# RWKV attention and two MLP layers: weights converted a slot at a time, bonus diagonals and decay clamp on GpSimd, and a new order of the first 24 steps

## The chip, the cores and the metric

The kernel runs on one core of a Trainium2 chip. The metric is device time in microseconds (us), one launch, everything from the first instruction to the last store. TensorE is called PE below, VectorE DVE, ScalarE ACT, GpSimd POOL, and SyncE's queue, which issues every DMA here, SP.

## The reference

A recurrent attention (4 batches, 8 heads, 768 tokens, head size 48) feeds a gated layer (384 to 1536 to 384) and then a squared-ReLU layer (384 to 2048 to 384), over 3072 tokens:

```python
for t in range(S):
    cur = einsum('bhd,bhe->bhde', u[None] * kt, vt)
    y[:, :, t] = einsum('bhd,bhde->bhe', rt, state + cur)
    state = wt[:, :, :, None] * state + einsum('bhd,bhe->bhde', kt, vt)
x = y laid out as (B*S, H*D)
x = (sigmoid(x @ w_gate) * (x @ w_val)) @ w_out
h = x @ w_in
out = (relu(h) ** 2) @ w_out2
```

The weights arrive as 64-bit floats in memory (the kernel sees pairs of 32-bit words); tokens and decays are float32.

## The kernel before

**Attention by chunks.** Each batch is cut into 6 chunks of 128 tokens, so there are 24 chunks; four of them (one of each batch) make a group of 512 tokens, and there are six groups. The steps of a chunk have one letter each in the order that the kernel keeps: L loads it (two DMAs, `att` with r, k and the decays w, `tok` with r, k, v by token); S is the scan on DVE (L318 clamps the decays in place, L319 and L324 are the two prefix scans, L327 scales r and k); B multiplies r, k and u on POOL (L342, L343); R sums that by head on DVE (L349) and writes eight diagonal 128x128 matrices on ACT (L355); A makes the r-k products on PE (L379) and copies their triangle over the diagonals on DVE (L382); K transposes k (L363, L368); D decays the carried state (L334, L337); Y makes the output on PE (L394, L400) and splits it into a high and a low half (L62, L63); U updates the state (L414, L421); G counts decays out of bounds on ACT (L300).

**First layer.** For each group there are 12 steps f, numbered through from 0 to 71. Step i has P (gate projection, 9 matmuls of 128x512 columns on L427 to L429, then the sigmoid on ACT, L457), Q (value projection, 9 matmuls, the product on DVE, L462, and its rounded copy on ACT, L463), l (the low half on DVE, L467) and M (9 matmuls into three accumulators). All products are made three times, with high and low halves of weights and data.

**Weights.** The 12 slots of weights w0 to w11 hold three parts of 384 columns each, high and low. Before, a part is a unit: 36 units, each loaded into one of 4 `raw` buffers (L154). A tick (letter T) of the stream runs, for three units at different stages: on ACT an Abs with a sum and a Relu with a sum (L166, L167, which count values out of bounds; each is followed by a reading of the accumulator); on DVE three integer instructions that put a float32 together out of the two words (L176, L181, L186); and the split, a rounding copy on ACT (L137) and a subtraction on POOL (L138). P of step i needs unit 3i, Q unit 3i+1, M unit 3i+2. Slots w7 to w11 first serve as space for chunks 2 and 3.

**Second layer's weights** are 32 units: stream s2 (ticks t) converts them in groups 2 to 4 in the same way (here with a clamp, L163 and L174) and stores them to memory as float32; r ticks in group 5 load them back and split them.

**Order.** Every engine runs its queue in program order, and that order is written by hand: the text START lists the steps for chunks 0 to 12 and f steps 0 to 23, and `steady` lists those of the other groups. In `steady` a chunk's B comes behind a Q, its scan behind the l that follows, its R at the end of that f step, and A and K behind the next Q. At the start SP issues chunks 0 to 3 with the first three weight units between them (L492 to L503).

Of the kernel before, what the change touches and what calls it, by code (L numbers as in the profile page):

```python
# [16 lines left out]
C = 128  # L17
# [18 lines left out]
    S0 B0 s0 T W19 R0 A0 S1 G0 T B1 K0 Y0 B2 S2 T R1 A1 U0 K1 K2 R2 G1 U1 S3 L4 B3 U2 T Y1 A2 K3 R3 A3 T L5 Y2  # L36
    G2 Y3 G3 U3 S4 T B4 Z P0 T R4 Q0 G4 D4 T A4 P1 K4 l0 T Q1 T Y4 l1 U4 S5 T P2 L6 M0 T M1 B5 T K5 Q2 R5 T T
    P3 l2 T A5 D5 Q3 P4 M2 T T l3 T Q4 T l4 Y5 G5 T U5 M3 T P5 Q5 T M4 S6 P6 l5 T B6 T Q6 D6 P7 T R6 M5 L7 T
    A6 K6 Q7 l6 T Y6 T l7 U6 T T P8 M6 T Q8 P9 l8 G6 M7 B7 S7 T D7 Q9 M8 T R7 A7 T L8 T P10 Y7 K7 G7 Q10 l9
    P11 l10 T U7 B8 T S8 M9 Q11 D8 M10 l11 P12 R8 M11 L9 Q12 P13 A8 K8 l12 Q13 M12 Y8 l13 G8 S9 B9 D9 U8 P14  # L40
    Q14 M13 P15 Q15 l14 P16 l15 M14 Q16 L10 B10 l16 M15 R9 A9 K9 P17 G9 Q17 S10 Y9 U9 l17 R10 P18 M16 Q18 M17
    P19 D10 L11 G10 l18 A10 Q19 B11 S11 P20 D11 Y10 R11 l19 K10 M18 Q20 U10 P21 M19 G11 L12 Q21 l21 l20 A11
    B12 S12 P22 M20 Q22 Y11 l22 K11 P23 U11 M21 R12 Q23 l23 M22 L13
# [22 lines left out]
def rwkv_moe(tc, att, tok, vt, u, w1, w2, out):  # L66
# [3 lines left out]
    with ExitStack() as ctx:  # L70
# [18 lines left out]
        outside = sb.tile([128, 2 * len(ORDER) + 6 * F1], F32, name="outside")  # L89
        out_w, out_s, out_b = (  # L90
            outside[:, 0 : 2 * len(ORDER)],
            outside[:, 2 * len(ORDER) : 2 * len(ORDER) + 3 * F1],
            outside[:, 2 * len(ORDER) + 3 * F1 :],
        )
        junk = sb.tile([128, DM], F32, name="junk")
# [33 lines left out]
        def w_part(i, part):  # L129
            k = i // 3  # L130
            if k not in wtile:
                wtile[k] = sb.tile([128, 2, 3, DM], F32R, name=f"w{k}", tag=f"w{k}")
            return wtile[k][:, part, i % 3]

        def w_split(i, val, eng):
            hi = w_part(i, 0)
            nc.scalar.copy(hi, val)  # L137
            eng.tensor_tensor(out=w_part(i, 1), in0=val, in1=hi.bitcast(F32), op=ALU.subtract)  # L138

        class Unit:  # L140
# [6 lines left out]
            def __init__(self, src, done, note=None):  # L147
                self.src, self.done, self.note = src, done, note

            def load(self):  # L150
                shape, dt = ([128, DM, 2], I32) if wide else ([128, DM], F32)
                self.raw = sb.tile(shape, dt, name="raw", tag="raw", bufs=4)
                src = self.src.bitcast(I32).rearrange("p (a b) -> p a b", b=2) if wide else self.src
                nc.sync.dma_start(self.raw, src)  # L154

            def start(self):
                if not wide:
                    self.h = self.raw
                    return
                self.h = sb.tile([128, DM], F32, name="h", tag="h", bufs=4)  # L160
                high = self.raw[:, :, 1].bitcast(F32)
                if self.note is None:
                    nc.scalar.activation(self.h, high, AF.Abs)  # L163
                else:
                    n = slice(self.note, self.note + 1)
                    nc.scalar.activation(junk, high, AF.Abs, accum_out=out_b[:, n])  # L166
                    nc.scalar.activation(junk, junk, AF.Relu, bias=1.0, scale=-1.0 / TINY, accum_out=out_s[:, n])  # L167

            def step(self, n):
                if not wide:  # L170
                    return
                h, hi = self.h, self.h.bitcast(I32)
                if n == 0 and self.note is None:
                    nc.vector.tensor_scalar(out=h, in0=h, scalar1=TINY, scalar2=HUGE, op0=ALU.max, op1=ALU.min)  # L174
                elif n == 1:
                    nc.vector.tensor_scalar(  # L176
                        out=hi, in0=hi if self.note is None else self.raw[:, :, 1], scalar1=3, scalar2=0x3FFFFFFF,
                        op0=ALU.logical_shift_left, op1=ALU.bitwise_and,
                    )
                elif n == 2:  # L180
                    nc.vector.scalar_tensor_tensor(  # L181
                        out=hi, in0=self.raw[:, :, 0], scalar=29, in1=hi,
                        op0=ALU.logical_shift_right, op1=ALU.bitwise_or,
                    )
                elif n == 3:
                    nc.vector.scalar_tensor_tensor(  # L186
                        out=hi, in0=self.raw[:, :, 1], scalar=-0x40000000, in1=hi,
                        op0=ALU.bitwise_and, op1=ALU.bitwise_or,
                    )

        class Stream:


            def __init__(self, units, lag):
                self.u, self.n, self.k, self.lag = units, 0, 0, lag
# [6 lines left out]
            def tick(self):  # L202
                k, u, lag = self.k, self.u, self.lag
                if k >= len(u) + lag + 2:
                    return
                self.k += 1
                at = lambda n: [u[n]] if 0 <= n < len(u) else []
                for x in at(k - lag - 2):
                    x.done(x.h)
                self.fetch(k + 1)  # L210
                for x in at(k):
                    x.start()
                mid, old = at(k - lag), at(k - lag - 1)
                for x in mid:
                    x.step(0)
                for x in old:
                    x.step(2)
                for x in mid:
                    x.step(1)
                for x in old:  # L220
                    x.step(3)
                self.fetch(k + 3)

            def until(self, n):
                while self.k < min(n, len(self.u)) + self.lag + 2:
                    self.tick()

        def w1_unit(i, note=None):
            src = w1[i // 3, :, DM * (i % 3) : DM * (i % 3) + DM]
            return Unit(src, lambda h: w_split(i, h, nc.gpsimd), note)  # L230

        def w2_unit(i):
            return Unit(w2[i // 2, :, DM * (i % 2) : DM * (i % 2) + DM], lambda h: nc.sync.dma_start(w2f[i], h))

        s1 = Stream([w1_unit(i, i) for i in range(3 * F1)], 0)
        s2 = Stream([w2_unit(i) for i in range(2 * F2)] if wide else [], 1)

        class Refill:
# [5 lines left out]
            def tick(self):  # L244
                if self.k >= 2 * F2:
                    return
                for i in range(self.k, min(self.k + 3, 2 * F2)):
                    if i not in self.t:
                        self.t[i] = sb.tile([128, DM], F32, name="h", tag="h", bufs=4)
                        src = w2f[i] if wide else w2[i // 2, :, DM * (i % 2) : DM * (i % 2) + DM]  # L250
                        nc.sync.dma_start(self.t[i], src)
                w_split(self.k, self.t.pop(self.k), nc.gpsimd)
# [41 lines left out]

        def st_guard(i):
# [16 lines left out]
        def st_scan(i, p0, p1):  # L312
# [4 lines left out]
            wc = wz[:, fl].rearrange("p (a c) -> p a c", c=CW)[:, :, 1 : C + 1]  # L317
            nc.vector.tensor_scalar(out=wc, in0=wc, scalar1=W_LOW, scalar2=W_HIGH, op0=ALU.max, op1=ALU.min)  # L318
# [26 lines left out]
        def st_bonus2(i):  # L345
# [3 lines left out]
            nc.vector.reduce_sum(out=a0, in_=d["t"][:, 0:DM].rearrange("p (h e) -> p h e", e=D), axis=AX.X)  # L349
            if spare(i):  # L350
                d["am"] = [spare(i)[:, n : n + 512].rearrange("p (a b) -> p a b", b=C) for n in (0, 512)]
            else:
                d["am"] = [sb.tile([128, NP, C], F32, name=f"am{i}_{j}", tag=f"am{j}", bufs=1) for j in range(2)]
            for h in range(H):
                nc.scalar.mul(d["am"][h % 2][:, h // 2], ident, a0[:, h : h + 1])  # L355
# [166 lines left out]
        def load(i):  # L522
# [4 lines left out]
            S=lambda i: half(i, 0), s=lambda i: half(i, 1), D=st_decay, G=st_guard, A=st_a, K=st_kt, B=st_bonus, R=st_bonus2,  # L527
# [14 lines left out]
        def st_p(i):  # L542
            if i < F1:
                s1.until(3 * i + 1)
# [3 lines left out]
        def st_q(i):  # L548
            if i < F1:
                s1.until(3 * i + 2)  # L550
# [3 lines left out]
        def st_m(i):  # L554
            if i < F1:
                s1.until(3 * i + 3)
# [20 lines left out]
        def steady(g):  # L577

            work = [[[], [], [], []] for _ in range(F1 + 1)]
            if g + 1 < NG:  # L580
                n = len(GROUPS[g + 1])
                for j, i in enumerate(GROUPS[g + 1]):
                    k = F1 // n * j
                    if k > 0:
                        work[k - 1][1] += ["B", i]
# [8 lines left out]
                    if j == n - 1 and i + 1 < len(ORDER):  # L594
                        work[F1 - 1][1] += ["B", i + 1]
# [3 lines left out]
            for f in range(F1):  # L599
                if NG - 4 <= g < NG - 1:  # L600
                    work[f][3] += ["t", 0]
# [28 lines left out]
        class Slot2:  # L630
# [18 lines left out]
            def mix(self):  # L649
                hi, lo = w_part(2 * self.f + 1, 0), w_part(2 * self.f + 1, 1)  # L650
                b0, b1 = self.f == 0, self.f == F2 - 1
                for j in range(4):
# [5 lines left out]
                    if b1:  # L658
                        y = sb.tile([128, DM], F32, name="y", tag="h", bufs=4)
# [93 lines left out]
        def general():  # L753
            scan_attention()
            wtile.clear()
            again = Stream([w1_unit(i) for i in range(3 * F1)], 1)
# [28 lines left out]
def lay_out(i):  # L785
# [29 lines left out]
    w2 = np.concatenate([cols(i["moe2_w_in"], F2), np.asarray(i["moe2_w_out"]).reshape(F2, 128, DM)], 2)  # L815
# [21 lines left out]
```

## Time and profile before

| | us |
|---|---|
| median of 3 runs | 1056.22 (1054.44 to 1056.26) |
| the profiled execution | 1050.92 |
| its span | 1049.1 |
| mean granted PE clock in it | 0.971 of full speed |

The span is what the profile covers; the profiled execution took 1.8 us more than its span. In the profile, "busy" counts the time in which an instruction stands in an engine, its waiting for a memory port included. L numbers are lines of the kernel before.

### The profile page before, as it was taken

How to read it: one execution, taken by the hardware profiler on the slowest of the kernel's cores; microseconds unless marked ns; L12 is line 12 of the kernel's file. 1: busy time of each engine (PE TensorE's matmuls, PEld its weight loads, DVE VectorE, ACT ScalarE, POOL GpSimd, SP SyncE). 2: the span in 40 equal slices, each digit the busy share in tenths (PEclk: the TensorE clock that was granted, in tenths of full speed). 3: DMA queues.
4: the chain of work that ended last, by engine and by line, in shares of the span. 5: the costliest groups of instructions: out<-in, count | busy, mean ns of one | idle time of the engine just before them, and what ended most of it. 6: DMA issues, size and time to landing. Idle time of an engine off the chain costs nothing.

```text
span 1049.1 us, 15123 instructions
## 1 busy us (share of the span) xinstructions
PE 975.0 (93%) x6013; PEld 812.9 (77%) x6013; DVE 534.3 (51%) x858; ACT 430.5 (41%) x988; POOL 150.3 (14%) x128
## 2 busy tenths in 40 slices
PE   4678979999999999999998999999999999999996
PEld 3456757787877777777777888899999999989996
DVE  6787886455366676666662233333334334333332
ACT  3768764253433443344442343333333233333322
POOL 3245642200000110001000451000000000000000
PEclk6698999999999999999999999999999999999999
DMA  9644540312444343344412332001010010100001
GB/s 257 180 127 147 162 142 21 113 53 74 143 125 142 122 150 119 120 120 153 139 39 83 99 98 76 1 1 61 1 61 1 1 61 1 61 1 1 31 1 34
DMA packets 33056, 87.08 MB, mean 83 GB/s; under 512 B 3712, under 2 KB 15328, under 8 KB 32976
## 3 DMA queue, kind: packets, MB, share of 16 engines
q1 hardware_dynamic: 32976, 86.02, 26.7%
q8 instruction: 49, 0.80, 0.3%
q14 instruction: 31, 0.25, 0.1%
HBM read 70.28 MB, written 15.73 MB: 82 GB/s over the span
## 4 chain that ended last, share of the span: by engine, by line
PE 71%; DVE 13%; ACT 8%; issue 5%; POOL 2%; DMA 1%; SPq 0%; DVEq 0%; ACTq 0%; POOLq 0%
PE gv L427 10%; PE gv L429 10%; PE gv L428 9%; PE acc L657 5%; PE acc L655 5%; PE acc L656 5%; PE rot L428 3%; PE rot L429 3%; PE rot L427 3%; PE acc L427 3%; ACT am L355 3%; PE acc L428 3%; PE acc L429 3%; DVE cum L319 3%; DVE cum L324 2%
## 5 line engine op out<-in xcount | busy, mean ns | idle before, releaser
L427 PE MATMUL gv<-xh,w 128*128 128x512 f32 x432 | 174.3, 403 | 9.5 <-ACT sig L457 8.3
L429 PE MATMUL gv<-xh,w 128*128 128x512 f32 x432 | 171.4, 397 | 3.8 <-POOL w L138 3.8
L428 PE MATMUL gv<-xl,w 128*128 128x512 f32 x432 | 170.8, 395 | 0.0
L646 DVE TENSOR_TENSOR sig<-sig 128x512 f32<-128x512 f32 x96 | 66.4, 691 | 185.6 <-ACT sig L645 185.6
L462 DVE TENSOR_TENSOR sig<-gv,sig 128x512 f32<-128x512 f32 x72 | 49.6, 689 | 157.8 <-PE gv L429 113.8
L427 PEld LDWEIGHTS gv<-xh,w 128*128 128x128 f32 x432 | 81.7, 189 | 33.0 <-ACT sig L457 13.9
L138 POOL TENSOR_TENSOR w<-h,w 128x384 fp32r<-128x384 f32 x68 | 82.8, 1232 | 161.9 <-ACT w L137 155.2
L429 PEld LDWEIGHTS gv<-xh,w 128*128 128x128 f32 x432 | 81.7, 189 | 24.6 <-POOL w L138 5.4
L63 DVE TENSOR_TENSOR gl<-sig,gh 128x512 fp32r<-128x512 f32 x96 | 66.4, 692 | 65.9 <-PE rot L657 48.8
L657 PE MATMUL acc<-w,gl 128*128 128x384 f32 x288 | 96.8, 336 | 0.1
L655 PE MATMUL acc<-w,gh 128*128 128x384 f32 x288 | 96.7, 336 | 0.1
L656 PE MATMUL acc<-w,gh 128*128 128x384 f32 x288 | 96.6, 335 | 0.0
L428 PEld LDWEIGHTS gv<-xl,w 128*128 128x128 f32 x432 | 81.8, 189 | 18.1 <-DVE xl L63 0.3
L62 ACT CAST gh<-sig 128x512 fp32r<-128x512 f32 x96 | 59.6, 621 | 74.0 <-DVE sig L646 74.0
L427 PE MATMUL acc<-gh,w 128*128 128x512 f32 x216 | 89.6, 415 | 0.4 <-ACT gh L463 0.4
L463 ACT CAST gh<-sig 128x512 fp32r<-128x512 f32 x72 | 44.7, 620 | 105.0 <-DVE sig L462 103.3
L428 PE MATMUL acc<-gl,w 128*128 128x512 f32 x216 | 86.8, 402 | 0.7 <-DVE gl L467 0.5
L355 ACT ACTIVATE am<-ident,a 128x128 f32<-128x128 f32 x176 | 53.9, 388 | 81.5 <-DVE a L349 81.5
L429 PE MATMUL acc<-gh,w 128*128 128x512 f32 x216 | 86.1, 399 | 0.0
L342 POOL TENSOR_TENSOR t<-t 128x384 f32<-128x384 f32 x24 | 32.2, 1340 | 325.0 <-DMA t<-in_tok 301.1
L457 ACT ACTIVATE sig<-gv 128x512 f32<-128x512 f32 x72 | 42.5, 590 | 71.9 <-PE gv L429 70.0
L645 ACT ACTIVATE sig<-gv 128x512 f32<-128x512 f32 x48 | 28.8, 599 | 102.8 <-PE gv L429 102.8
(117 smaller groups left out, 1834.8 us busy)
## 6 DMA issues: line engine op xcount, KB each, us to landing
raw<-in_w SPq DMA_DIRECT2D x68, 384.0 KB, 3.5
a<-in_att SPq DMA_DIRECT2D x23, 675.5 KB, 5.7
t<-in_tok SPq DMA_DIRECT2D x24, 640.0 KB, 6.7
w2f<-h SPq DMA_DIRECT2D x32, 192.0 KB, 4.8
h<-w2f SPq DMA_DIRECT2D x32, 192.0 KB, 2.6
x2d<-x2o SPq DMA_DIRECT2D x18, 256.0 KB, 2.0
x2r<-x2d SPq DMA_DIRECT2D x6, 768.0 KB, 4.3
out<-y SPq DMA_DIRECT2D x24, 192.0 KB, 2.0
```

The source lines that it names most:

```text
L62: nc.scalar.copy(hi, src)
L63: nc.vector.tensor_tensor(out=lo, in0=src, in1=hi.bitcast(F32), op=ALU.subtract)
L138: eng.tensor_tensor(out=w_part(i, 1), in0=val, in1=hi.bitcast(F32), op=ALU.subtract)
L355: nc.scalar.mul(d["am"][h % 2][:, h // 2], ident, a0[:, h : h + 1])
L427: nc.tensor.matmul(o, w_hi, x_hi, start=start, stop=False)
L428: nc.tensor.matmul(o, w_hi, x_lo, start=False, stop=False)
L429: nc.tensor.matmul(o, w_lo, x_hi, start=False, stop=stop)
L462: nc.vector.tensor_tensor(out=self.s[:, :n], in0=gv[1][:, :n], in1=self.s[:, :n], op=ALU.mult)
L646: nc.vector.tensor_tensor(out=r, in0=r, in1=r, op=ALU.mult)
L655: nc.tensor.matmul(o, self.gh[:, cs], hi, start=b0, stop=False)
L656: nc.tensor.matmul(o, self.gh[:, cs], lo, start=False, stop=False)
L657: nc.tensor.matmul(o, self.gl[:, cs], hi, start=False, stop=b1)
```

## The change

Seven edits in one:

- a unit of the first stream is a whole slot (1152 columns): 12 units. The raw words are loaded into the slot's own place (`raw` with the tag of the slot), converted into an `h` of 1152 columns, and split back into the slot: one copy on ACT, three subtractions on POOL;
- a tick is a third of a unit: a (first DVE instruction; it also begins with the split of the unit before), b (second one, then the Abs on ACT, which now writes over the low words), c (third one, then the Relu on ACT). P of step i needs the whole slot; Q and M ask for nothing more. The stream loads 4 units ahead;
- stream s2 keeps 384 columns with 2 raw buffers in place of 4, three ticks per unit, and three ticks per f step in place of one;
- the clamp of the decays becomes a step C on POOL (for chunk 0 it stays on DVE);
- the eight diagonals of a chunk are made by one `affine_select` on POOL from the sums, in place of eight ACT instructions;
- START is rewritten; `steady` places C at the beginning of the f step whose later quarters hold B, S and R;
- small buffers: 384-column tiles of w2, refill and output share tiles of three; the second layer's weights are laid out unit by unit in memory.

The diff, cut to its core:

```diff
-    S0 B0 s0 T W19 R0 A0 S1 G0 T B1 K0 Y0 B2 S2 T R1 A1 U0 K1 K2 R2 G1 U1 S3 L4 B3 U2 T Y1 A2 K3 R3 A3 T L5 Y2
-    G2 Y3 G3 U3 S4 T B4 Z P0 T R4 Q0 G4 D4 T A4 P1 K4 l0 T Q1 T Y4 l1 U4 S5 T P2 L6 M0 T M1 B5 T K5 Q2 R5 T T
...
-    P11 l10 T U7 B8 T S8 M9 Q11 D8 M10 l11 P12 R8 M11 L9 Q12 P13 A8 K8 l12 Q13 M12 Y8 l13 G8 S9 B9 D9 U8 P14
...
+    W19 B0 S0 C1 s0 R0 K0 B1 A0 R1 U0 S1 T C2 T S2 Y0 B2 K2 G0 T L4 G1 R2 C3 A1 A2 K1 T B3 S3 U1 Y1 T U2 R3 L5
+    A3 Y2 C4 T B4 Y3 K3 U3 G3 Z T S4 R4 P0 G4 Q0 K4 P1 T D4 T A4 Q1 C5 U4 T T l0 l1 S5 G2 T P2 Y4 M0 B5 T D5 T
...
+    K6 T T l6 R6 M5 P7 T A6 T T Q7 L7 T C7 l7 U6 P8 T M6 Q8 l8 P9 T B7 M7 S7 Y6 T G6 Q9 D7 R7 T L8 A7 T G7 M8
+    K7 P10 l9 T Y7 Q10 C8 l10 M9 U7 P11 B8 Q11 l11 M10 L9 M11 P12 T S8 R8 Q12 A8 K8 D8 l12 P13 Q13 P14 B9 Y8
...
+            def a(self):
...
+                nc.vector.tensor_scalar(
+                    out=i, in0=i if self.note is None else self.hi, scalar1=3, scalar2=0x3FFFFFFF,
+                    op0=ALU.logical_shift_left, op1=ALU.bitwise_and,
+                )
+            def b(self):
...
+                nc.vector.scalar_tensor_tensor(
+                    out=i, in0=self.lo, scalar=29, in1=i, op0=ALU.logical_shift_right, op1=ALU.bitwise_or
+                )
+                if self.note is not None:
+                    n, junk = slice(self.note, self.note + 1), self.lo.bitcast(F32)
+                    nc.scalar.activation(junk, self.hi.bitcast(F32), AF.Abs, accum_out=out_b[:, n])
...
             def tick(self):
+                k, part = divmod(self.k, 3)
+                if self.k > 3 * len(self.u):
                     return
                 self.k += 1
+                if part == 0:
+                    self.fetch(k + 1)
+                    if k:
+                        self.u[k - 1].d()
+                    if k < len(self.u):
+                        self.u[k].a()
+                    self.fetch(k + self.ahead)
+                elif part == 1:
+                    self.u[k].b()
+                else:
+                    self.u[k].c()
...
+            def raw():
+                return sb.tile([128, 3 * DM, 2], I32, name=f"raw{f}", tag=f"w{f}")
+            def split(h):
+                w = w_slot(f)
+                nc.scalar.copy(flat(w[:, 0]), h)
+                for n in range(3):
+                    cs = slice(DM * n, DM * n + DM)
+                    nc.gpsimd.tensor_tensor(
+                        out=w[:, 1, n], in0=h[:, cs], in1=w[:, 0, n].bitcast(F32), op=ALU.subtract
+                    )
...
+        s1 = Stream([w1_unit(f, f) for f in range(F1)], 4)
+        s2 = Stream([w2_unit(i) for i in range(2 * F2)] if wide else [], 2)
...
+        def st_clamp(i, p0=0, p1=NP, eng=None):
+            wc = chunk[i]["w"].rearrange("p (a c) -> p a c", c=CW)[:, p0:p1, 1 : C + 1]
+            (eng or nc.gpsimd).tensor_scalar(out=wc, in0=wc, scalar1=W_LOW, scalar2=W_HIGH, op0=ALU.max, op1=ALU.min)
...
-            wc = wz[:, fl].rearrange("p (a c) -> p a c", c=CW)[:, :, 1 : C + 1]
-            nc.vector.tensor_scalar(out=wc, in0=wc, scalar1=W_LOW, scalar2=W_HIGH, op0=ALU.max, op1=ALU.min)
+            if i == 0:
+                st_clamp(i, p0, p1, nc.vector)
...
-            for h in range(H):
-                nc.scalar.mul(d["am"][h % 2][:, h // 2], ident, a0[:, h : h + 1])
+            nc.gpsimd.affine_select(
+                out=am, in_=a0.unsqueeze(2).to_broadcast([128, H, C]),
+                compare_op=ALU.is_equal, fill=0.0, base=0, pattern=[[0, H], [-1, C]], channel_multiplier=1,
+            )
...
             if i < F1:
-                s1.until(3 * i + 1)
+                s1.until(3 * i + 3)
...
+                        work[k - 1][0] += ["C", i]
                         work[k - 1][1] += ["B", i]
                         work[k - 1][2] += ["S", i]
                         work[k - 1][3] += ["R", i]
...
-                    work[f][3] += ["t", 0]
+                    for q in (0, 2, 3):
+                        work[f][q] += ["t", 0]
```

## Rows read from the trace of the kernel before

**Rows 1.** The page's first part: busy time, share and instructions of each engine.

```profile
span 1049.1 us, 15123 instructions
PE 975.0 (93%) x6013; PEld 812.9 (77%) x6013; DVE 534.3 (51%) x858; ACT 430.5 (41%) x988; POOL 150.3 (14%) x128
```

**Rows 2.** By stage: busy us (instructions) of PE, PEld, DVE, ACT, POOL; clock; DMA.

```profile
0.00:50.00 50.00, 27.13 (x292) 20.16 (x292) 35.40 (x56) 26.68 (x81) 15.80 (x23) 0.62 0.78 223
50.00:180.00 130.00, 107.96 (x719) 82.06 (x719) 101.01 (x172) 89.95 (x262) 64.56 (x43) 0.95 0.40 121
180.00:270.00 90.00, 85.92 (x666) 68.28 (x665) 45.84 (x69) 35.05 (x86) 11.69 (x10) 1.00 0.26 82
270.00:563.00 293.00, 278.53 (x2005) 220.36 (x2004) 184.24 (x324) 119.04 (x291) 24.11 (x20) 0.99 0.39 122
```

**Rows 3.** DVE timeline: one chunk's scan in group 2, undisturbed, and its neighbours.

```profile
366.06 0.69 DVE L467 TENSOR_TENSOR gl<-sig,gh 128x512 fp32r<-128x512 f32 x1 [0.69 <-ACT gh L463]
366.67 0.42 DVE L318 TENSOR_SCALAR a<-a 112x512 f32<-112x512 f32 x1
367.13 1.24 DVE L319 TENSOR_TENSOR_SCAN cum<-a,inj 112x520 f32<-112x520 f32 x1
368.62 1.24 DVE L324 TENSOR_TENSOR_SCAN cum<-a,inj 112x520 f32<-112x520 f32 x1
369.90 1.22 DVE L327 TENSOR_TENSOR a<-a,cum 112x1024 f32<-112x1024 f32 x1
...
371.77 0.55 DVE L181 SCALAR_TENSOR_TENSOR h<-raw,h 128x384 int32<-128x384 int32 x1
372.24 0.35 DVE L176 TENSOR_SCALAR h<-h 128x384 int32<-128x384 int32 x1
```

**Rows 4.** What PE waited for from 270 to 563 us: total, times, longest.

```profile
PE rot L379 <- DVE a L327: 12.8, 11, 1.8
```

**Rows 5.** POOL timeline, 100 to 140 us, two instructions of 384 columns.

```profile
116.08 5.00 POOL L342 TENSOR_TENSOR t<-t 128x384 f32<-128x384 f32 x1
...
127.24 1.00 POOL L138 TENSOR_TENSOR w<-h,w 128x384 fp32r<-128x384 f32 x1 [1.64 <-DVE am L382]
```

**Rows 6.** DVE groups from 50 to 180 us, shapes apart.

```profile
L181 DVE SCALAR_TENSOR_TENSOR h<-raw,h 128x384 int32<-128x384 int32 x32 | 19.3, 604 | 0.0
L176 DVE TENSOR_SCALAR h<-raw 128x384 int32<-128x384 int32 x31 | 14.1, 454 | 2.7 <-POOL w L138 2.7
```

**Rows 7.** ACT groups from 50 to 180 us, shapes apart.

```profile
L166 ACT ACTIVATE junk<-raw 128x384 f32<-128x384 f32 x31 | 17.1, 553 | 0.0
L137 ACT CAST w<-h 128x384 fp32r<-128x384 f32 x33 | 16.7, 506 | 15.3 <-DVE h L186 15.2
L167 ACT ACTIVATE junk<-junk 128x384 f32<-128x384 f32 x31 | 16.3, 525 | 1.0
L355 ACT ACTIVATE am<-ident,a 128x128 f32<-128x128 f32 x40 | 12.2, 388 | 2.7 <-DVE a L349 2.6
```

**Rows 8.** Groups of the whole run, shapes apart: long forms, memset and select.

```profile
L63 DVE TENSOR_TENSOR xls<-x2r,xhs 128x1536 fp32r<-128x1536 f32 x6 | 10.6, 1758 | 5.9 <-ACT xhs L62 5.9
L62 ACT CAST xhs<-x2r 128x1536 fp32r<-128x1536 f32 x6 | 8.8, 1473 | 0.0
L122 POOL MEMSET block<- 112x384 f32 x2 | 0.8, 420 | 0.0
masks.py:199 POOL TENSOR_SCALAR_AFFINE_SELECT ident<-ident 128x128 f32<-128x128 f32 x1 | 0.3, 292 | 0.0
```

**Rows 9.** POOL timeline, 0 to 32 us: the bonus of chunk 3 begins.

```profile
30.09 1.37 POOL L342 TENSOR_TENSOR t<-t 128x384 f32<-128x384 f32 x1 [3.05 <-DMA t<-in_tok]
```

**Rows 10.** PE timeline from 46 us: the first matmul of P0.

```profile
49.92 0.50 PE L427 MATMUL gv<-xh,w 128*128 128x512 f32 x1
```

**Rows 11.** DMA issues of the weight units: count, KB each, us to landing.

```profile
raw<-in_w SPq DMA_DIRECT2D x68, 384.0 KB, 3.5
```

**Rows 12.** Stage of 10 to 20 us, columns as in rows 2; the last is GB/s.

```profile
10.00:20.00 10.00, 2.54 (x32) 1.56 (x32) 5.94 (x8) 6.99 (x22) 2.88 (x3) 0.50 1.02 272
```

More of the change, by code (lines that the diff above doesn't have):

```diff
@@ L127, in rwkv_moe, with w_slot @@
         wide = w1.dtype != F32
-        def w_part(i, part):
-            k = i // 3
+        def w_slot(k):
             if k not in wtile:
                 wtile[k] = sb.tile([128, 2, 3, DM], F32R, name=f"w{k}", tag=f"w{k}")
[L133 to L138, printed above, removed]
+            return wtile[k]
@@ L140, in rwkv_moe, with w_part, third, __init__ @@
+        def w_part(i, part):
+            return w_slot(i // 3)[:, part, i % 3]
+        thirds = []
+        def third():
+            if not thirds:
+                t = sb.tile([128, 3, DM], F32, name="h3", tag="h", bufs=2)
+                thirds.extend(t[:, n] for n in range(3))
+            return thirds.pop(0)
         class Unit:
-            def __init__(self, src, done, note=None):
-                self.src, self.done, self.note = src, done, note
+            def __init__(self, n, src, raw, h, done, note=None):
+                self.n, self.src, self.get_raw, self.get_h, self.done, self.note = n, src, raw, h, done, note
@@ L169, in step @@
-            def step(self, n):
+                if wide:
+                    self.raw = self.get_raw()
+                    self.hi, self.lo = self.raw[:, :, 1], self.raw[:, :, 0]
+                    src = self.src.bitcast(I32).rearrange("p (a b) -> p a b", b=2)
+                    nc.sync.dma_start(self.raw, src)
+                else:
+                    self.h = self.get_h()
+                    nc.sync.dma_start(self.h, self.src)
+            def a(self):
                 if not wide:
                     return
-                h, hi = self.h, self.h.bitcast(I32)
-                if n == 0 and self.note is None:
+                h = self.h = self.get_h()
+                i = h.bitcast(I32)
+                if self.note is None:
+                    nc.scalar.activation(h, self.hi.bitcast(F32), AF.Abs)
@@ L191, in rwkv_moe, with d, __init__ @@
+            def d(self):
+                self.done(self.h)
         class Stream:
-            def __init__(self, units, lag):
-                self.u, self.n, self.k, self.lag = units, 0, 0, lag
+            def __init__(self, units, ahead):
+                self.u, self.n, self.k, self.ahead = units, 0, 0, ahead
             def fetch(self, n):
@@ L232, in w2_unit @@
         def w2_unit(i):
-            return Unit(w2[i // 2, :, DM * (i % 2) : DM * (i % 2) + DM], lambda h: nc.sync.dma_start(w2f[i], h))
-        s1 = Stream([w1_unit(i, i) for i in range(3 * F1)], 0)
-        s2 = Stream([w2_unit(i) for i in range(2 * F2)] if wide else [], 1)
+            raw = lambda: sb.tile([128, DM, 2], I32, name="raw", tag="raw", bufs=2)
+            return Unit(DM, w2[i], raw, third, lambda h: nc.sync.dma_start(w2f[i], h))
+        s1 = Stream([w1_unit(f, f) for f in range(F1)], 4)
@@ L658, in mix @@
                     if b1:
[L659 removed]
+                        y = third()
                         if j % 2:
@@ L755, in general @@
             wtile.clear()
-            again = Stream([w1_unit(i) for i in range(3 * F1)], 1)
+            again = Stream([w1_unit(f) for f in range(F1)], 2)
             again.until(3 * F1)
```

115 lines of the change are left out of this document (41 added, 74 removed).

## The prediction

> **What bounds the kernel now.** I read the page's first part first: PE is busy for 975 us of the span, DVE for half of it, POOL for 14% [rows 1]. A share over the whole run does not say where there is something to win, so the stages come next [rows 2]. P0 begins at 49.9 us [rows 10], the first 12 f steps run until about 180, those of group 1 until about 270, groups 2 to 4 until about 563; what follows is hardly touched by the change. Three things are to be seen. From 50 to 180 us PE is idle for 22 of 130 us, and DVE and POOL together are busy for 165.6 us of the 130. From 180 to 270 us PE is idle for only 4. From 270 to 563 us it is idle for 14.5, and the waits say that 12.8 of these are eleven waits for one thing, the end of a chunk's scan [rows 4].
>
> Why two engines that overlap count together is in the third view. A POOL instruction of 384 columns takes 1.00 us by itself, and one that met DVE's queue running without a gap took 5.00 [rows 5]; on DVE the same conversion instruction takes 0.55 us alone and 0.60 on average in this stage, its neighbour 0.35 alone and 0.45 [rows 3, 6]. So I take DVE's and POOL's work on SBUF as one queue there, and its demand at undisturbed lengths is: 64 word instructions of 0.55 (35.2), 31 shifts of 0.35 (10.9), five chunks' scans and scalings of 1.24 + 1.24 + 1.22 (18.5), five clamps of 0.42 (2.1), twelve low halves of 0.69 (8.3), 43 POOL instructions of 1.00 (43.0) [rows 2, 3, 5, 6]. The sum is 118.0 us, 91% of the 130. This, not PE, sets the stage.
>
> A page of the Trainium skill puts it as a rule: "SBUF — State Buffer", section "Who interferes with whom", says that VectorE and GpSimd share one pair of ports, that the pair goes to one of them for a whole instruction, and that VectorE takes it with two SBUF inputs or in its two-port mode. The 5.00 beside 1.00 agrees.
>
> **The change part by part.** Conversion, on DVE. A slot needs one instruction where there were three. What a longer one costs I take from another two-input instruction, 1.758 us for 1536 columns against 0.55 for these 384: 1.05 ns a column, so 0.55 becomes 0.55 + 768 x 0.00105 = 1.36 [rows 3, 8]. The shift goes by 0.35 at 384 against 0.42 at 512 (the clamp, same kind), 0.55 ns a column, so 0.77 [rows 3]. Seven ticks stand ahead of P0 in the new order, which are two slots; before they were six ticks, four units. Ten slots remain, 10 x (2 x 1.36 + 0.77) = 34.9 us against 46.1: -11.2. Subtractions stay as they are, 30 against 33 by then.
>
> Chunks. The fifth scan of this stage, chunk 8's, now stands behind M11; group 1, where it goes, has DVE busy for half the time [rows 2], which covers it: -3.7 here and nothing there. If that cover were gone it would cost the 3.7. The clamps leave DVE: -2.1.
>
> POOL. The bonus of four chunks is in the stage, as before within one. No row shows the two new kinds. The clamp of 512 columns lies between 0.55 us (0.86 ns a column, from 0.42 for a memset of 384 and nothing more than that) and 1.33 (the two-input 1.00 for 384); it has one input, so it is nearer to the lower end and I take 0.8. The select of 1024 columns lies between 1.0 (the memset's rate) and 2.3 (eight times the 0.29 of the 128-column select in the setup); part of that 0.29 is paid once, so 1.6. With 30 subtractions, 8 bonus instructions, 4 clamps and 4 selects POOL's part is 30 + 8 + 3.2 + 6.4 = 47.6 us against 43.0: +4.6 [rows 2, 5, 8].
>
> So the common queue has 118.0 - 11.2 - 3.7 - 2.1 + 4.6 = 105.6 us, and at the same 91% the stage takes 116: **-14 us**. At the ends of the two prices, 4 x (0.55 + 1.0) or 4 x (1.33 + 2.3), it is -17 or -8; PE's idle 22 us is the limit, since a stage cannot gain more than PE stands still.
>
> ACT. 31 pairs at 0.553 and 0.525 and 33 copies at 0.506 cost 50 us, and 40 diagonals 12.2 [rows 7]. At no more than 0.96 ns a column (1.473 for 1536 [rows 8]), ten slots cost at most 10 x (0.553 + 0.525 + 0.506 + 3 x 768 x 0.00096) = 38 us, a third as many accumulator readings come on top, and the diagonals cost nothing, so ACT falls from 90 to at most 66 us of 130. I count no gain for it: ACT waited for the queue above (15.2 us for conversions alone [rows 7]). It gets one new wait: the Abs writes over the low words, so it stands in ACT's queue until DVE has done b, and behind it stand the sigmoid and the rounded copy on which PE's next P waits. It lengthens single f steps and is one reason why I don't go to the 22.
>
> Before P0. SP puts three units of 1152 columns between the first four chunks where there were three of 384: 3 x 0.79 = 2.36 MB more [rows 11], at 272 GB/s 8.7 us [rows 12]. These loads wait for nothing, and slot 3's follows the chunks. Chunk 3's bonus would begin at 38.8 us instead of 30.1 [rows 9]. But from there to P0 there were 19.8 us, in which DVE was also busy with ticks; the chain itself (bonus 2.0, sum 0.5, select 1.6, triangles 1.4, Y 2.5, split 1.0, and one word instruction of 1.36 between) is some 11. P0 then begins at about 50 or 51: **+1**. Bounds: -2, if the chain is tighter, and the full +8.7.
>
> Groups 2 to 4. PE's eleven waits of 1.16 us end with L327. Ahead of it on DVE stand the low half, the clamp and two scans [rows 3, 4]; without the clamp L327 ends 0.46 earlier (0.42 and the gap behind it): 11 x 0.46 = **-5**. C stands a Q ahead of B on POOL, which by then has waited for `tok`, loaded behind `att`; so C is done and delays nobody. Late next is the gated product's chain, then PE itself. Bounds: 0, if POOL's bonus takes the port that the clamp left, and -12.8. The selects fall behind R, when DVE has only ticks, and A's triangles come two instructions later; the ACT time saved there was not waited for. Three t ticks per f step instead of one do the same work; the store of a unit moves on SP to the next f step's beginning, behind a load that was issued before it, and two raw buffers suffice because each load has an f step to land in 3.5 us [rows 11]. Refill and output: nothing, their buffers come free as many ticks ahead as before.
>
> Sum: -14 + 1 - 5 = -18 us. The profiled execution took 1050.9 (1.8 more than its span), 5.3 less than the median of 1056.2; I set the difference against the median: **1038**, which would be 1033 for that execution.
>
> **The rivals.** (1) POOL becomes the late one. The clamp now stands ahead of the scan and the select ahead of A's triangles; both queue behind DVE's unbroken runs. A wait of 4.0 us, as in the row of 5.00, for the select of the seven chunks 1 to 7 would add 28 us: 1038 + 28 = **1066**, slower. It decides from 18 / 7 = 2.6 us per chunk. For it: that row. Against it: ACT's eight diagonals took as long before (8 at some 0.3 apart), and there is a step or two between R and A. In the skill it is "Perfetto Trace Analysis", section "Optimizing Scalar/DVE Operations": moving work between GPSIMD and DVE might not help, for the shared read port. (2) The stage is a chain, not a queue: PE, ACT and DVE wait for each other in turn, with longer instructions in each queue, so the 12 us of demand saved shift into waits and the first stage gains 3; with -5 and +1: **1049**. (3) The first loads decide: P0 is late by the 8.7 and begins at the half clock that was granted from 10 to 20 us [rows 12], some 2 us more; 1038 + 7.7 + 2 = **1048**. (4) The work is taken off where nothing waits: the port keeps the scan late in groups 2 to 4, and the start gives back what it wins: **1056**, no difference.
>
> **How the numbers follow.** The forecast, with its own range of 1022 (22 in the first stage, 10 of the 12.8, 2 before P0) to 1053 (-5, 0, +2), has 0.58. Rival 2 has 0.12, rival 3 0.07, both faster; rival 4 0.08; rival 1 0.15. A difference of 0.2%, 2.1 us, is what a measurement here can tell. So faster 0.77, same 0.08, slower 0.15. The range of 1020 to 1057 holds all but rival 1 and some of the forecast's own low end.
>
> **What would show it.** Right: conversions (the last subtraction) end some 14 us earlier, at 155 to 160 us; POOL's select takes 1 to 2.3 us, its clamp 0.5 to 1.4; PE's waits for L327 in groups 2 to 4 fall by 5 us; P0 within 2 us of 50. Wrong: PE or DVE waiting for the select or the clamp for over 2 us per chunk; P0 near 59 us; PE's idle time from P0 to M11 still some 22 us though DVE's is up.

## The result and the profile after

The kernel after takes 1029.32 us, median of 4 runs (1028.43 to 1032.59), against 1055.33 for the kernel before in the same comparison: a ratio of 0.9765, 95% interval 0.9734 to 0.9796, so 2.35% faster. The forecast was 18 us less; it is 26 by the medians and 21.7 by the two profiled spans (1049.1 and 1027.4).

The first part of the page and the stages, which answer to [rows 1] and [rows 2]:

```profile
span 1027.4 us, 14742 instructions
PE 967.2 (94%) x6013; PEld 809.0 (79%) x6013; DVE 541.7 (53%) x763; ACT 363.8 (35%) x676; POOL 226.6 (22%) x175
```

```profile
0.00:50.00 50.00, 22.25 (x239) 16.83 (x239) 32.44 (x40) 12.74 (x27) 27.91 (x29) 0.63 0.89 286
50.00:180.00 130.00, 115.58 (x845) 88.55 (x849) 106.74 (x112) 74.09 (x131) 88.21 (x58) 0.95 0.32 111
270.00:563.00 293.00, 284.06 (x2023) 225.38 (x2013) 194.59 (x315) 95.84 (x203) 59.42 (x47) 1.00 0.39 126
```

ACT lost 67 us of work over the run, POOL gained 76, and DVE is busy for longer although it has 95 instructions fewer. The stages have moved against each other, so the clearest account goes by events. P0's first matmul is in PE's timeline, and the first store of each group's output in SP's. From them, in us, for every kernel of this study (each from its own profiled execution, with the median of its runs; a column is the time between two such events, and the experiments below say what each kernel is):

| kernel | P0 begins | P0 to first store | group 1 | groups 2 to 4 | after that | median |
|---|---|---|---|---|---|---|
| before | 49.9 | 127.5 | 98.2 | 292.5 | 481.0 | 1055.3 |
| after | 57.8 | 108.7 | 98.1 | 280.6 | 482.1 | 1029.3 |
| before + small POOL instruction | 50.5 | 127.9 | 101.7 | 281.4 | 485.0 | 1046.0 |
| before + select | 48.5 | 122.7 | 97.4 | 276.4 | 482.8 | 1028.9 |
| before + clamp on POOL | 50.0 | 128.9 | 100.0 | 284.9 | 482.7 | 1050.3 |
| before + new order | 60.1 | 123.2 | 98.4 | 292.7 | 483.3 | 1056.3 |
| after, diagonals on ACT | 62.1 | 113.5 | 98.7 | 297.5 | 484.2 | 1052.9 |
| the same + small POOL instruction | 59.7 | 112.3 | 98.5 | 287.1 | 483.7 | 1044.1 |
| after, old order | 55.0 | 136.9 | 97.3 | 279.5 | 484.2 | 1053.0 |
| after, clamp on DVE | 56.7 | 110.3 | 98.1 | 281.7 | 481.8 | 1030.4 |
| after, later weight loads | 57.4 | 108.6 | 97.9 | 280.9 | 483.9 | 1030.5 |
| after, POOL's first steps moved | 54.8 | 112.9 | 97.9 | 280.6 | 484.4 | 1031.5 |
| after, t ticks together | 58.7 | 109.7 | 98.5 | 273.2 | 481.9 | 1023.8 |
| after, both of these | 55.2 | 111.5 | 97.7 | 274.1 | 485.0 | 1023.7 |

The medians come from four comparisons, in which the kernel before took 1055.3, 1053.5, 1051.7 and 1052.7 us; each ratio below is against the kernel before of the same comparison. Kernels that share the code of groups 2 to 4 repeat that column (279.5 to 280.9 for four of them, 292.5 and 292.7, 273.2 and 274.1), while the last column spreads over 4 us although hardly anything differs there.

The change begins P0 8 us later, runs the first 12 f steps 19 us faster, and takes 12 us off groups 2 to 4. The last of these was the surprise. The waits of PE from 265 to 546 us, which answer to [rows 4]:

```profile
PE gv L462 <- DVE sig L497: 4.2, 10, 0.7
...
PE rot L414 <- DVE a L356: 1.7, 2, 1.0
```

Of the 12.8 us that PE waited for the scans' ends, 1.7 are left, and 4.2 of another wait have come, for the gated product. Groups 2 to 4 as a stage, before and after:

```profile
275.60:568.10 292.50, 275.40 (x1979) 217.62 (x1978) 183.53 (x325) 117.32 (x287) 24.11 (x20) 0.99 0.40 122
264.70:545.30 280.60, 271.65 (x1979) 215.19 (x1978) 192.88 (x313) 92.48 (x198) 53.27 (x41) 1.00 0.39 125
```

PE's idle time fell from 17.1 to 9.0 us; the other 3.8 of the 11.9 are its busy time for the same matmuls, at a mean granted clock of 0.99 before and 1.00 after. One chunk in group 2, DVE and POOL together:

```profile
374.03 0.69 DVE L502 TENSOR_TENSOR gl<-sig,gh 128x512 fp32r<-128x512 f32 x1 [0.69 <-ACT gh L498]
374.64 1.23 DVE L348 TENSOR_TENSOR_SCAN cum<-a,inj 112x520 f32<-112x520 f32 x1
...
376.13 1.24 DVE L353 TENSOR_TENSOR_SCAN cum<-a,inj 112x520 f32<-112x520 f32 x1
377.40 1.22 DVE L356 TENSOR_TENSOR a<-a,cum 112x1024 f32<-112x1024 f32 x1
...
379.01 0.55 DVE L378 TENSOR_REDUCE a<-t 128x8 f32<-128x384 f32 x1
...
379.70 1.28 POOL L387 TENSOR_SCALAR_AFFINE_SELECT am<-a 128x1024 f32<-128x1024 f32 x1 [18.86 <-DVE a L378]
...
379.94 1.24 DVE L363 TENSOR_TENSOR S<-S,cum 112x192 f32<-112x192 f32 x1
...
381.06 1.92 POOL L322 TENSOR_SCALAR a<-a 112x512 f32<-112x512 f32 x1
...
383.06 1.02 POOL L371 TENSOR_TENSOR t<-t 128x384 f32<-128x384 f32 x1
```

POOL's next bonus starts only behind the select, and the select only behind the sums, so nothing of POOL is left in the time of the scan. In the kernel before, POOL's waits in these groups show that its bonus began, nine times of ten, when its load had landed:

```profile
POOL t L342 <- DMA t<-in_tok: 197.3, 9, 24.2
```

and in the kernel after they show one releaser:

```profile
POOL am L387 <- DVE a L378: 205.5, 11, 25.7
```

Chunk by chunk, the timeline of the kernel before shows what this does. For nine of the eleven chunks a bonus instruction lengthened the low half, the clamp or a scan, and PE then waited 1.1 to 1.8 us for the scan's end; for the other two, one of them the undisturbed chunk of [rows 3], it waited 0.3 to 0.4. A disturbed one and that one:

```profile
297.30 0.71 PE L379 MATMUL rot<-a 48*128 48x128 f32 x8 [1.83 <-DVE a L327]
...
371.18 0.60 PE L379 MATMUL rot<-a 48*128 48x128 f32 x6 [0.32 <-DVE a L327]
```

That gave the theories: the **queue theory** (POOL's queue is held back by the select, and the bonus leaves the scan's time), the **ACT theory** (ACT without the diagonals is what PE gained from) and the **clamp theory** (the clamp that left DVE, which was mine).

### The profile page after: what moved, and what is told of

Same layout as the page of the kernel before. It is cut to its first block, busy times and chain, and to the rows that moved or that the text cites. A ratio compares the mean times of both kernels' runs of the same rounds, so it can differ in the third digit from the quotient of the medians.

```text
span 1027.4 us, 14742 instructions
## 1 busy us (share of the span) xinstructions
PE 967.2 (94%) x6013; PEld 809.0 (79%) x6013; DVE 541.7 (53%) x763; ACT 363.8 (35%) x676; POOL 226.6 (22%) x175
## 4 chain that ended last, share of the span: by engine, by line
PE 71%; DVE 13%; issue 5%; POOL 4%; ACT 3%; DMA 2%; SPq 0%; DVEq 0%; ACTq 0%; POOLq 0%
PE gv L462 10%; PE gv L464 9%; PE gv L463 9%; PE acc L691 5%; PE acc L689 5%; PE acc L690 5%; PE rot L463 3%; PE rot L464 3%; PE rot L462 3%; PE acc L462 3%; PE acc L463 3%; PE acc L464 3%; DVE cum L353 2%; DVE cum L348 2%; DMA a<-in_att 2%
## 5 line engine op out<-in xcount | busy, mean ns | idle before, releaser
L63 DVE TENSOR_TENSOR gl<-sig,gh 128x512 fp32r<-128x512 f32 x96 | 66.5, 693 | 65.9 <-PE rot L691 37.1
L387 POOL TENSOR_SCALAR_AFFINE_SELECT am<-a 128x1024 f32<-128x1024 f32 x22 | 28.5, 1297 | 277.3 <-DVE a L378 277.3
L462 PE MATMUL acc<-gh,w 128*128 128x512 f32 x216 | 88.5, 410 | 0.0
L464 PE MATMUL acc<-gh,w 128*128 128x512 f32 x216 | 84.8, 393 | 0.0
L502 DVE TENSOR_TENSOR gl<-sig,gh 128x512 fp32r<-128x512 f32 x72 | 55.9, 778 | 20.5 <-ACT gh L498 20.5
L679 ACT ACTIVATE sig<-rot 128x512 f32<-128x512 f32 x48 | 28.8, 600 | 93.0 <-PE rot L464 92.6
```

Source lines behind the costliest of these rows:

```text
L63: nc.vector.tensor_tensor(out=lo, in0=src, in1=hi.bitcast(F32), op=ALU.subtract)
L462: nc.tensor.matmul(o, w_hi, x_hi, start=start, stop=False)
L464: nc.tensor.matmul(o, w_lo, x_hi, start=False, stop=stop)
L502: nc.vector.tensor_tensor(out=self.gl[:, :n], in0=self.s[:, :n], in1=self.gh[:, :n].bitcast(F32), op=ALU.subtract)
L679: nc.scalar.activation(r, self.h, AF.Relu)
```

## The experiments

**A small POOL instruction in the kernel before.** It only holds the queue.

```diff
             nc.vector.reduce_sum(out=a0, in_=..., axis=AX.X)
+            gate = sb.tile([128, H], F32, name=f"gate{i}", tag="gate", bufs=1)
+            nc.gpsimd.tensor_tensor(out=gate, in0=a0, in1=a0, op=ALU.mult)
```

> The kernel before, with one POOL instruction of 8 columns added behind R's sums, which reads them: POOL's queue then cannot begin the next chunk's bonus until the sums are done, that is until the scan is over. Queue theory (in groups 2 to 4 the new kernel won 12 us because its select holds POOL's queue back, so the bonus no longer meets the scan at the port): the scans fall from 1.44 and 1.32 us to 1.24 each and the clamp from 0.79 to 0.42, 0.65 us per chunk or 7 us over eleven; groups 2 to 4, from the second to the fifth store of a group, 292.5 to about 285.5, in all some 1048. Clamp theory (the clamp that left DVE won it) and ACT theory (ACT freed of the diagonals won it): nothing in groups 2 to 4, 1055 in all or some us more, since POOL's subtractions in the first group also queue behind the added instruction.

Measured: 1046.01 us, ratio 0.993 (0.9907 to 0.9953); groups 2 to 4 at 281.4, 11 less, where 7 were expected. The first scan and the clamp in the kernel before (276 to 568 us):

```profile
L319 DVE TENSOR_TENSOR_SCAN cum<-a,inj 112x520 f32<-112x520 f32 x11 | 15.9, 1442 | 0.4
...
L318 DVE TENSOR_SCALAR a<-a 112x512 f32<-112x512 f32 x11 | 8.7, 788 | 0.0
```

PE's waits and the same two with the small instruction (280 to 561 us), two views:

```profile
PE rot L381 <- DVE a L327: 3.5, 11, 0.4
```

```profile
L319 DVE TENSOR_TENSOR_SCAN cum<-a,inj 112x520 f32<-112x520 f32 x11 | 13.7, 1242 | 0.4
...
L318 DVE TENSOR_SCALAR a<-a 112x512 f32<-112x512 f32 x11 | 4.6, 420 | 0.0
```

Scan and clamp have their undisturbed lengths, with the clamp still on DVE and the diagonals still on ACT. The queue theory holds: 9.3 of the 12.8 us of PE's wait are gone. The expectation counted the scans and the clamp and left out the low half, which in four chunks of the kernel before took 0.83 to 1.54 us instead of 0.69. Four us are given back ahead of the second store, where the first groups' steps queue behind the same instruction, so the whole run gains 7.5 us.

**Select alone and clamp alone, in the kernel before.**

```diff
-            for h in range(H):
-                nc.scalar.mul(d["am"][h % 2][:, h // 2], ident, a0[:, h : h + 1])
+            nc.gpsimd.affine_select(out=am, in_=a0.unsqueeze(2).to_broadcast([128, H, C]), ...)
```

> The kernel before with the diagonals made by the select on POOL and nothing else. Queue theory: groups 2 to 4 fall by about 7 us to 285.5, as with the small instruction alone. ACT theory: by 10 or more. Clamp theory: by nothing. In the first group ACT loses 12 us of work and the common port gains some 6: between 3 us faster and 3 slower. In all 1045 to 1051 by the queue theory.

```diff
-            nc.vector.tensor_scalar(out=wc, in0=wc, scalar1=W_LOW, scalar2=W_HIGH, op0=ALU.max, op1=ALU.min)
+            if i == 0:
+                st_clamp(i, p0, p1, nc.vector)
```

> The kernel before with the clamp of chunks 1 to 23 on POOL, just ahead of the scan or the bonus of its chunk in the first order, and at the beginning of the f step in groups 2 to 4. Clamp theory: groups 2 to 4 fall by 5 to 12 us from 292.5. Queue theory: POOL is not held back, so clamp (1.92 us) and bonus run as their loads land, in the scan's time as before: between 3 us less and 4 more. In the first group the port has 1.5 us more per chunk: 0 to 8 us more. In all 1052 to 1064 by the queue theory, 1044 to 1052 by the clamp theory.

Beside the lines shown, the sums of the select's kernel are written in the order that the select reads, and the clamp's kernel has the step C in both orders.

The select alone: 1028.93 us, ratio 0.9766 (0.9729 to 0.9802). **That is the whole gain of the change**, from one of its edits. Groups 2 to 4 fall by 16.1, 5 more than with the small instruction, so ACT's time counts there too, and the first store comes 6.2 earlier. With the small instruction PE's weight loads (PEld) still wait for ACT's sigmoid in groups 2 to 4, as they do in the kernel before (5.5 us in 9 waits); with the select they have no such wait:

```profile
PEld gv L429 <- ACT sig L459: 6.5, 11, 0.9
```

Over the whole run the two kernels are 17.1 us apart, of which the profiles put 7.1 ahead of the first store and 4.3 in group 1. So of the select's 24.6 us the queue accounts for some 7.5, all of it in groups 2 to 4, and the larger part comes from making the diagonals on POOL instead of ACT. My expectation, 1045 to 1051, was too high by 16 us and more.

The clamp alone: 1050.27, ratio 0.997 (0.9949 to 0.9991), groups 2 to 4 by 7.7 less, more than the queue theory allowed and within the clamp theory. The disturbance did stay, as the first scan shows (279 to 563 us):

```profile
L316 DVE TENSOR_TENSOR_SCAN cum<-a,inj 112x520 f32<-112x520 f32 x11 | 16.0, 1455 | 0.0
```

PE's wait for the scans' ends is 7.8 us there. So two things shorten the same wait of 12.8 us, the clamp's absence and the undisturbed scan. They don't add up: with the select in place the clamp's side is worth 1 us (below).

**The change without the select, and with the small instruction in its place.** Both put the eight ACT instructions back; the second adds the two lines of the first experiment.

> The new kernel with the diagonals back on ACT. Queue theory: nothing holds POOL's queue back, clamp and bonus run when their loads land and meet the scan: groups 2 to 4 rise from 280.6 us by 5 to 12, the scans from 1.24 us to 1.4 or more; in all 1035 to 1045. ACT theory: groups 2 to 4 rise by 10 as well, but the scans stay at 1.24. Clamp theory: groups 2 to 4 stay at 281. In the first group ACT has 12 us more: 0 to 5 us more.

> The new kernel with the diagonals back on ACT, and a POOL instruction of 8 columns that reads the sums where the select stood. Queue theory: POOL is held back as by the select, so groups 2 to 4 stay within 2 us of 280.6 although ACT makes the diagonals again. ACT theory: they rise by 5 to 12 us, as without the small instruction. In all 1029 to 1035 by the queue theory, 1035 to 1045 by the ACT theory.

Without the select: 1052.91 us, ratio 0.9997 (0.9975 to 1.0019). **All other edits together gain nothing**, the spread of the t ticks, which costs time (below), among them. PE's waits and the first scan from 275 to 571 us:

```profile
PE rot L413 <- DVE a L356: 12.8, 10, 2.6
```

```profile
L348 DVE TENSOR_TENSOR_SCAN cum<-a,inj 112x520 f32<-112x520 f32 x11 | 19.3, 1753 | 0.0
```

The scans are worse than before: a bonus instruction now lies in the time of a scan for ten of the eleven chunks, where it was three in the kernel before. On POOL's queue it now stands behind the clamp. With the small instruction: 1044.06, ratio 0.9927 (0.99 to 0.9955), scans at 1.23 again, groups 2 to 4 at 287.1. I had expected 280.6 within 2: of the 16.9 us between the two versions the queue gives 10.4, and the other 6.5 come with the diagonals on ACT, where DVE's conversions wait longer for ACT's Abs (63.9 us against 42.6):

```profile
DVE h L173 <- ACT h L172: 63.9, 27, 3.9
```

In groups 2 to 4 both theories hold a part, and the larger one is the queue's. Over the whole run it is the other way round, as in the kernel before: the ratios 0.9997, 0.9927 and 0.9765 give 0.7% to the queue and 1.6% to the diagonals' move from ACT to POOL. How much of that is ACT's time and how much diagonals that are ready sooner (one select against eight ACT instructions) was not separated.

**The clamp back on DVE.**

```diff
-            if i == 0:
-                st_clamp(i, p0, p1, nc.vector)
+            st_clamp(i, p0, p1, nc.vector)
```

> The new kernel with the clamp of every chunk back on DVE. It took 1.92 us on POOL when nothing disturbed it, against 0.42 on DVE. Groups 2 to 4: the clamp stands ahead of the scan again, 11 x 0.46 = 5 us more than 280.6. First group: the port is free for 1.5 us more per chunk and DVE's scan waits for nothing from POOL; by my sum over the port 4 chunks give 4 x (1.92 - 0.42) = 6 us. In all 1026 to 1032. If the clamp on POOL is what won groups 2 to 4: 10 us more there, 1033 to 1039.

Measured: 1030.35, ratio 0.9802 (0.9779 to 0.9825), no difference that the intervals separate; groups 2 to 4 lose 1.1, the first store comes at 167.1 instead of 166.5. Neither my 5 nor my 6 us came. In groups 2 to 4 PE waits longer for the scans' ends (5.4 us instead of 1.7), but its wait for the gated product falls from 4.2 to 0.5.

**The order.** The kernel after with the old START (C ahead of its chunk's bonus or scan), and the kernel before with the new one.

> The new kernel with the order of the first 24 f steps of the kernel before; C is put just ahead of the bonus or scan of its chunk. If conversion by slots and the engines' new shares win the first group's 19 us by themselves, P0 to M11 stays within 4 us of 108.7 us and the time within 5 of 1029. If the new order is what makes them usable (a slot's three ticks now have to be ended ahead of P, not of M), P0 to M11 rises by 10 to 25 us, 1040 to 1055 in all.

> The kernel before with the new order of the first 24 f steps (its step C does nothing there: the clamp stays on DVE). If the new order is better by itself, P0 to the first group's stores falls from 127.5 us towards 115 and the time to 1038 to 1046. If it only fits units of a whole slot (ticks are thirds of a slot there, and P, not M, needs the slot's end), 1049 to 1062.

The old order with whole slots: 1053.0, ratio 1.0017 (0.9993 to 1.0041); P0 to the first store takes 136.9 us, 28 more than with the new order. What PE waits for from 55 to 192 us:

```profile
PE gv L455 <- ACT w L238: 16.9, 6, 7.0
```

P waits for the slot's split, which the old order puts too late. The new order with the old units: 1056.31, ratio 1.0036 (1.001 to 1.0061), so it is no gain by itself. The two belong together, and together they bring the first store from 171.2 (select alone) to 166.5 us, 4.7 earlier, of which the clamp on POOL, also in this difference, is at most 0.6.

**Why P0 is late.** My bound for it was the weight loads between the first chunks.

```diff
         load_tok(1)
-        s1.fetch(2)
...
-        s1.fetch(3)
```

> The new kernel with slots 1 and 2 (2.36 MB) loaded behind chunks 0 to 3 instead of between them. If the first loads set P0 (57.8 us against 49.9 before the change), chunk 2 and chunk 3 land 4 and 8 us earlier and P0 begins at 50 to 53 us; in all 1022 to 1026. If the order of the steps or the port sets it, P0 stays at 56 to 59 us and the time at 1028 to 1031.

Measured: 1030.47, ratio 0.9798 (0.9773 to 0.9824), P0 at 57.4. The loads are not the cause. The chain that ended last in the kernel after, ahead of P0:

```profile
41.66 5.23 POOL w L248 x3
46.89 2.10 POOL t L371
49.06 1.01 POOL t L372
50.09 0.57 DVE a L378
50.79 1.09 POOL room L387
51.90 0.73 DVE room L417
52.68 2.53 PE acc L435 x32
```

It runs through POOL's queue: slot 0's three subtractions, then chunk 3's bonus, its sums, its select, Y. So POOL's steps were moved:

```diff
-W19 B0 S0 C1 s0 R0 ... R2 C3 A1 A2 K1 T B3 S3 U1 Y1 T U2 R3
+W19 B0 S0 s0 R0 C1 ... R2 C3 B3 A1 A2 K1 S3 R3 U1 Y1 T T U2
```

> The new kernel with POOL's first steps in another order: R0 ahead of C1, B3 ahead of the first slot's subtractions, R3 ahead of them too. POOL-queue theory: P0 is late (57.8 us) because chunk 3's bonus and select stand behind the first slot's three subtractions on POOL, 5.2 us, and chunk 0's select behind chunk 1's clamp, which waits for its load: P0 begins at 52 to 55 us, and if the first group gives nothing back the time is 1023 to 1027. Port theory: conversions end when they end, so M11's stores stay at 166.5 us and the time at 1028 to 1031, wherever P0 begins.

In this kernel and in the one with both edits (the table's last row) R3 stands ahead of Y1; chunks 1 and 3 share the space `room`, so chunk 1's output is made with chunk 3's diagonals, and neither is a version to use. The instructions are the same, but Y1 now has to wait for chunk 3's select. Measured: 1031.5, ratio 0.9789 (0.9767 to 0.9812). P0 begins at 54.8, as the POOL-queue theory said, and the first store comes at 167.7, as the port theory said. The port theory is right: an earlier P0 is worth nothing, since the last subtraction ends at 160.1 us (158.8 without the move). The POOL-queue theory holds for 3.0 of the 7.9 us by which P0 is late, and that figure is not clean, because PE waited for the misplaced select:

```profile
PE gv L428 <- POOL room L380: 5.0, 1, 5.0
```

The rest is not POOL's queue alone: the new order in the kernel before, with none of the new POOL work, has P0 at 60.1 us, and the old order with all the other edits has it at 55.0. What the order and the larger units add was not separated.

**A better version: the t ticks together.** Groups 2 to 4 take 280.6 us in the kernel after, 276.4 with the select alone. What DVE waited for there in the kernel after (265 to 546 us):

```profile
DVE h L173 <- ACT h L172: 42.6, 27, 3.8
```

```diff
-                    for q in (0, 2, 3):
-                        work[f][q] += ["t", 0]
+                    work[f][3] += ["t", 0] * 3
```

> The new kernel with the three t ticks of an f step in its last quarter instead of one each in the first, third and last. Wait theory: spread out, DVE's first conversion instruction stands in its queue waiting for ACT's Abs (42.6 us in 27 waits from 265 to 546 us) ahead of the gated product that frees PE's bank; in the last quarter ACT has long done it, so groups 2 to 4 fall from 280.6 to 276 or 277 us, as long as with the select alone in the kernel before (276.4), and the time to 1024 to 1026. Buffer theory: the two raw buffers or the shared tiles of three cost these 4 us: no change, 1028 to 1031.

> The new kernel with both: the t ticks in the last quarter and POOL's first steps in the other order. If both theories hold, 4 us less in groups 2 to 4 and 3 to 5 less ahead of P0: 1019 to 1023. If only the wait theory holds: 1024 to 1026.

Measured: 1023.8 us, ratio 0.9725 (0.9703 to 0.9747); groups 2 to 4 at 273.2, 7.4 less. PE's waits there (265 to 541 us):

```profile
PE rot L338 <- DVE tot L336: 2.6, 1, 2.6
PE rot L414 <- DVE a L356: 2.0, 4, 0.7
```

The wait for the gated product is gone, and DVE's wait for the Abs fell from 42.6 us to 19.1, so the wait theory holds. This version beats the kernel before; its interval and that of the kernel after overlap a little, but its groups 2 to 4 are shorter by far more than that column varies. With POOL's steps moved as well: 1023.7, ratio 0.9715 (0.9688 to 0.9742), no more than with the ticks alone. Beside the select, the other edits with the ticks together are worth some 5 us (1028.9 against 1023.8), though the intervals of the two ratios overlap.

## Why the prediction was right, and where its steps were not

The sign, the size within its range and two of the places were right. Point by point:

- **The sum, in part luck.** Its two large terms, -14 for the conversions and the port and -5 for the clamp, come to nothing without the select (ratio 0.9997): no difference, as rival 4 had it. The select alone gains 24.6 us, and the sum carries it as a cost on POOL and as no gain on ACT. So the forecast was met in large part by a term that is not in it.
- **Conversion and port, -14 us: nearly right, by another split.** The last subtraction ends at 158.8 us instead of 170.8, so 12 earlier; 14 were forecast. From P0 to the first store it is 18.8 less, 7.9 of that because P0 is later. The lengths of the long instructions were right as well (1.35 us and 0.75 undisturbed, forecast 1.36 and 0.77). But the saving did not arrive as a sum over the port says: beside the select, slots and the new order are worth 4.7 us at the first store, without it the stage is 14.0 shorter but P0 12.2 later, so that the first store gains 1.9, near the 3 of rival 2, and the whole run nothing; and with the old order slots lose. The select gives the larger part there, 6.2 in the kernel before.
- **ACT, counted at no gain: wrong.** "ACT waited for the queue above" was true of its waits, but ACT's 12 us of diagonals stood in its queue ahead of sigmoids. Putting them back, with the small instruction to hold POOL's queue as before, moves the first store from 166.5 to 172.0 (P0 1.9 later, the stage 3.6 longer), and costs 6.5 us in groups 2 to 4. ACT's work was also undercounted: it was busy for 74 us from 50 to 180, not for 66 at most.
- **P0, +1 us: wrong in size.** It was +7.9, near the 8.7 that I kept as a bound, but not because of the loads. The chain itself was right, some 11 us from chunk 3's bonus (46.9 us) to P0 (57.8). The step that failed is its start: I had the bonus begin at 38.8, when its load lands, and left out what stands ahead of it on POOL. Rival 3's late P0 came, and so did its half clock, but its cause, the loads, is excluded, and its price did not show: the first store came 10.9 us earlier all the same. The clock behind P0 (the column of 0.51 and 1.00), after and before:

```profile
57.80:60.70 2.90, 2.90 (x8) 2.32 (x8) 2.80 (x4) 2.71 (x6) 0.00 (x0) 0.51 0.57 159
...
49.90:53.00 3.10, 3.10 (x14) 2.34 (x13) 3.00 (x5) 3.04 (x11) 1.17 (x2) 1.00 0.38 116
```

- **Groups 2 to 4, -5 us: right wait, wrong cause, half the size.** It was -11.9. I priced the wait of 1.16 us by the row of an undisturbed chunk, behind which PE waited only 0.32; the mean comes mostly from the nine chunks that the bonus disturbed. "The selects fall behind R, when DVE has only ticks" was right, and I priced it at nothing; that a select which waits for R also holds back the bonus queued behind it I did not see, though I had asked only who waits for the select and not what is queued behind it. The bound of -12.8 came close.
- **Three t ticks "do the same work": wrong.** DVE's first instruction of each unit now met ACT's Abs too early; that cost 4 to 7 us.
- **Prices on POOL.** The clamp takes 1.92 us where nothing disturbs it, above my upper end of 1.33; the select takes 1.09, near my lower end of 1.0. Together they came to 3.0 per chunk against my 2.4. (My lower ends went by 0.86 ns a column; a memset of 0.42 us for 384 columns is 1.09, which makes them 0.56 and 1.12.) In the first stage, beside DVE, both took longer; POOL's groups from 57.8 to 166.5 us:

```profile
L248 POOL TENSOR_TENSOR w<-h,w 128x384 fp32r<-128x384 f32 x33 | 47.2, 1459 | 26.6 <-ACT w L245 26.6
L322 POOL TENSOR_SCALAR a<-a 112x512 f32<-112x512 f32 x4 | 10.3, 2582 | 0.3
...
L387 POOL TENSOR_SCALAR_AFFINE_SELECT am<-a 128x1024 f32<-128x1024 f32 x4 | 6.3, 1583 | 2.4 <-DVE a L378 2.4
```

- **The rivals.** POOL did not become the late one where it matters: DVE waits for the select for 0.4 us in all in groups 2 to 4, for 2.0 from P0 to the first store, and for 7.8 once at the start, for chunk 0's, which stands behind chunk 1's clamp. The rule in the Trainium skill, "Perfetto Trace Analysis", section "Optimizing Scalar/DVE Operations", that work moved between GPSIMD and DVE might not help, fits the clamp: beside the select, the time is 1029.3 us with it on POOL and 1030.4 with it on DVE, no difference that the intervals separate.

## What to carry to other kernels

Where two engines lengthen each other's instructions, what matters is not only how much work each has but when its queue lets it run: an instruction that waits for the right event keeps everything behind it out of the critical engine's time, and one such instruction of 8 columns was worth 11 us in a stage here, 7.5 in all. Work that is taken off an engine can pay even where that engine seems only to wait: the diagonals' move from ACT to POOL gave some 17 us more. When a change has several edits, try each by itself in the kernel before; one of seven gave everything here, and one took some 5 us back. A price of nothing for a moved instruction needs the list of what stands behind it on its queue.

## What was not expected of the hardware

On POOL, a clamp with two constants took 1.92 us for 512 columns, 3.75 ns a column, and a select from eight values spread over 1024 columns took 1.09, 1.06 ns a column; a two-input product of 384 columns took 1.00, 2.6 ns a column. The number of columns says little without the kind. The decay of the state on DVE, 0.35 us alone (112x192), took 1.24 beside the select (the row at 379.94 us), so the instruction that now runs beside POOL's pays. And the product of 1.00 us that took 5.00 [rows 5] was held for longer than one instruction: nine of DVE's began in its time, one behind the other without a gap (117.12 to 120.74 us).
